# Sigmoid attention and a seven-product MLP: operands and decoding placed anew, 27 rounding copies on ScalarE, one PSUM tile for each bank

## The chip, the cores and the metric

The kernel runs on one core of one Trainium2 chip. The metric is device time in microseconds for one execution of the whole program; the time given for a kernel is the median of its runs. The engines are called as in the profile: PE (TensorE, matmuls), PEld (its weight loads), DVE (VectorE), ACT (ScalarE), POOL (GpSimd) and SP (SyncE, which here issues the DMAs).

## What is computed

Eight batches of 12 heads with 448 tokens and head size 64 go through attention with a sigmoid in place of a softmax; the result, as 3584 tokens of width 768, goes through two linear layers with a gate between them. All arrays are float32.

```
scores = (q @ k.T) / sqrt(64) - log(448)
x      = (1 / (1 + exp(-scores))) @ v          # per batch and head, then [3584, 768]
h      = x @ w_in                              # [3584, 2048]
g      = h * clip(h + 3, 0, 6) / 6
out    = g @ w_out                             # [3584, 768]
```

## The kernel before

**Stages.** Tokens are taken as four pairs of batches, n = 0 to 3. The program runs attention for batches 0 to 3, the first product (`x @ w_in`) for pair 0, attention for batch 4, product for pair 1, attention for batches 5 and 6, product for pair 2, attention for batch 7, product for pair 3, and then the second product (`g @ w_out`) for all four pairs.

**Products.** Each big product is split in two in every dimension and done with seven block products in place of eight; in the code they are P1, P5, P6, P2, P7, P3, P4, and this is also their order in time. Every float32 operand is split in a rounded part and a rest (two tiles of type fp32r), and a block product is three passes over these: high by high, high by low, low by high. One call of `product` is nine matmuls of 448 columns.

**Token operands.** `take` (L219) adds the two PSUM halves of one head pair into a raw tile `xr` (ACT copies one half, DVE adds the other). `put` (L228) makes one operand of the first product from a raw tile: L230 rounds it into x[:, 0], L231 subtracts to get the rest into x[:, 1]. `minus` (L234) is a difference of two raw tiles. For each pair n and each of three columns c, `t_ops` (L237) places seven puts and four differences, with b11, b12, b21, b22 the four raw tiles. In before all of them run on DVE.

**Decoding of weights.** `w_in` and `w_out` arrive as 64-bit numbers. `prep` (L91) decodes one of eight blocks of either (`which` 0 or 1) in two units: a load, an ACT step `head` (L108), five DVE steps (L113 to L123), an add on POOL (L127); then four sums on POOL and seven stores to a DRAM scratch. So there are 32 units. `split_w` (L261) reads weights back (`raw` tiles), rounds them on ACT (L264) and subtracts on DVE (L265).

**One quarter of a first product.** `quads` (L276) runs the seven products for two column blocks i = 0, 1 and four quarters jj. On the way, `seed` (L303, ACT) copies the P1 bank into the P2 bank before P6 goes on adding to P1; `keep` (L307, ACT) saves P5; `seed2` (L311, DVE) writes the P3 bank, and P7 may add to P1 only after it; `h22` (L315, DVE) makes the tile `snh`, and P4 may add to P1 only after it. `gate` (L327, ACT) and `gate2` (L330, DVE) turn four results into g11, g22, g12 and g21; `diff` (L335, DVE) makes the four differences t1 to t4; all are stored for the second product.

**PSUM.** There are eight banks of 512 columns. Four are the tiles pv0 to pv3 (`bank`, L86). The other four are two tiles of two banks each, sc0 and sc1 (`pair_banks`, L80): in attention one step's scores fill such a pair. In the first product each of the four roles P1, P5, P2, P3 needs two banks, one for each i; which role has which banks turns with jj. Two roles have single banks, and two have one pair tile, which holds both i:

```
m = (jj + (P1, P5, P2, P3).index(role)) % 4
if m % 2:
    return bank(f"z_{n}_{jj}_{role}_{i}", (m - 1) + i)
if role not in whole:
    whole[role] = pair_banks(f"z_{n}_{jj}_{role}", turn[0] + m // 2)
return whole[role][:, i]
```

Waits are made per tile, from the accesses that the program records on it.

**Order.** The order of the work is a list: `at(place, f, ...)` gives a step its place, in microseconds of a planned timeline, and the list is sorted by place. PE, DVE, ACT and POOL take their instructions in just that order, and each waits at its first instruction that isn't ready. SP's DMAs are ordered by the compiler's scheduler. In the plan, the four first products begin at places 136.0, 273.1, 443.0 and 580.1 (`marks`), attentions at 5.0, 240.4, 377.5 and 547.3 (`starts`).

Of the kernel before, what the change touches and what calls it, by code (L numbers as in the profile page):

```python
# [43 lines left out]
def tile_kernel(ctx: ExitStack, tc: tile.TileContext, qk, vP, w8, outT):  # L44
# [183 lines left out]
    def put(n, k, c, q):  # L228
        x = one.tile([P, 2, S], F32R, tag=f"x{k}{c}", name=f"x_{n}_{k}_{c}")
        nc.vector.tensor_copy(x[:, 0], xr[q])  # L230
        nc.vector.tensor_tensor(out=x[:, 1], in0=xr[q], in1=x[:, 0].bitcast(F32), op=ALU.subtract)  # L231
        X[n, k, c] = x
# [231 lines left out]
    for n, bs in enumerate(runs):  # L464
        steps = [(b, m, r) for b in bs for m in range(HC) for r in range(LC)]
        lag = 2
        starts.append(now)
# [21 lines left out]
    for n in range(NT):
        free = marks[n - 1] + HF * q if n else 0.0  # L490
        for c in range(HC):
            own = [taken[2 * n + (h % 2), c + HC * (h // 2)] for h in range(4)]
            late = 0.4 * c
            first = (max(free - 11.6 * TU + 1.1 * c, own[0] + late), max(free - 5.6 * TU + 1.1 * c, own[2] + late))
            upper = max(free - 9.6 * TU + 1.7 * c + 0.5, own[1] + late, first[0] + 0.1)
            if max(own) < free:
                both = free - 0.5 + 7 * c
                t_ops(n, c, (first, upper, both), 0.9)
# [62 lines left out]
```

## Time and profile before

| | us |
|---|---|
| runs | 1140.26, 1143.6, 1144.16 |
| median | 1143.6 |
| profiled execution: time | 1146.25 |
| profiled execution: span | 1144.5 |
| PE busy | 1101.1 (96%) |
| DVE busy | 832.2 (73%) |
| ACT busy | 609.8 (53%) |
| POOL busy | 147.3 (13%) |

How to read it: the span is the time from the first to the last instruction. Matmuls are pipelined, so PE counts as busy while any is under way, also when its clock is throttled; the granted clock (PEclk) is a number of its own. A view of groups gives, for each line and form, the count, the busy time, the mean duration in ns of one, and the idle time of the engine just before, with what ended it. A view of waits gives, for each pair of waiter and releaser, the microseconds in total, the times, and the longest. Names in it are without their numbers: z is a PSUM tile of the first product, y and yb those of the second, sc and pv those of attention, x an operand, w a split weight.

### The profile page before, as it was taken

Reading aid. Unit: us, or ns where it says so; the run is one execution under the profiler, and the core shown is the slowest. Engines: PE = TensorE matmul, PEld = TensorE weight load, DVE = VectorE, ACT = ScalarE, POOL = GpSimd, SP = SyncE. Lnnn points to the kernel's source line nnn. Section 1 sums busy time; section 2 is a strip of 40 time slices with the busy share of each in tenths; the row PEclk is TensorE's granted clock in tenths of the full one; section 3 lists DMA queues with packets and bytes.
Section 4 is the critical chain, followed back from the end, with each engine's and each line's share of the span. In section 5 each row is a group of like instructions: output and inputs, shape, how many; then the busy total and the mean of one; then the engine's idle time right before and its main releaser. Section 6 shows DMA issues by size and latency. Waiting matters only on the chain.

```text
span 1144.5 us, 17865 instructions
## 1 busy us (share of the span) xinstructions
PE 1101.1 (96%) x6720; PEld 888.9 (78%) x6720; DVE 832.2 (73%) x1128; ACT 609.8 (53%) x814; POOL 147.3 (13%) x102
## 2 busy tenths in 40 slices
PE   8989999988899989999989999999999999999998
PEld 3436688983488854699854989999999999999997
DVE  4897688999589889668797786856655665665563
ACT  6857844536544457745437354554455445445542
POOL 0533443201212202021130000000000000000000
PEclk9999999989899999999999999999999999999999
DMA  7877899774779767678853987394543453355341
GB/s 267 274 261 252 278 319 312 256 248 179 228 234 301 237 229 239 220 242 265 282 179 115 361 282 227 131 419 169 174 178 125 142 188 131 121 171 170 124 147 68
DMA packets 95270, 250.22 MB, mean 219 GB/s; under 512 B 10576, under 2 KB 66256, under 8 KB 90704
## 3 DMA queue, kind: packets, MB, share of 16 engines
q1 hardware_dynamic: 95040, 249.01, 63.8%
q8 instruction: 53, 0.87, 0.3%
q14 instruction: 33, 0.27, 0.1%
q10 hardware_dynamic: 144, 0.07, 0.0%
HBM read 164.63 MB, written 84.41 MB: 218 GB/s over the span
## 4 chain that ended last, share of the span: by engine, by line
PE 69%; DVE 18%; issue 5%; DMA 4%; ACT 4%; SPq 0%; ACTq 0%; DVEq 0%
PE y L408 24%; PE z L297 19%; PE yb L408 12%; PE sc L188 7%; PE pv L214 6%; DVE w L265 3%; DMA raw<-wd 2%; DVE t L335 2%; DVE x L231 2%; DVE x L230 2%; DVE xr L235 2%; DVE g L330 2%; ACT w L264 1%; PE sc L183 1%; PE pv L208 1%
## 5 line engine op out<-in xcount | busy, mean ns | idle before, releaser
L297 PE MATMUL z<-x,w 128*128 128x448 f32 x2016 | 423.5, 372 | 15.7 <-ACT z L305 7.9
L297 PEld LDWEIGHTS z<-x,w 128*128 128x128 f32 x2016 | 383.4, 191 | 57.1 <-issue 10.8
L408 PE MATMUL y<-x,w 128*128 128x448 f32 x1344 | 308.0, 364 | 0.0
L408 PEld LDWEIGHTS y<-x,w 128*128 128x128 f32 x1344 | 252.0, 187 | 19.9
L265 DVE TENSOR_TENSOR w<-w,w 128x768 fp32r<-128x768 f32 x112 | 107.3, 958 | 153.8 <-ACT w L264 152.5
L194 ACT ACTIVATE a<-sc,bias_s 128x896 f32<-128x896 f32 x168 | 168.9, 1008 | 71.6 <-PE sc L188 39.2
L264 ACT CAST w<-w 128x768 fp32r<-128x768 f32 x112 | 93.4, 834 | 190.8 <-PE yb L408 187.1
L188 PE MATMUL sc<-qk 64*64 64x448 f32 x1152 | 174.8, 557 | 10.0 <-DVE g L330 5.3
L214 PE MATMUL pv<-a,v 64*64 64x448 f32 x1152 | 174.8, 548 | 9.0 <-DVE xr L223 7.6
L408 PE MATMUL yb<-x,w 128*128 128x448 f32 x672 | 172.3, 364 | 0.0
L265 DVE TENSOR_TENSOR w<-raw,w 128x768 fp32r<-128x768 f32 x112 | 126.4, 1132 | 44.5 <-ACT w L264 41.9
L408 PEld LDWEIGHTS yb<-x,w 128*128 128x128 f32 x672 | 126.0, 187 | 9.9
L127 POOL TENSOR_TENSOR wa<-wa,st 128x768 f32<-128x768 f32 x32 | 64.4, 2012 | 448.3 <-DVE st L123 374.3
L391 DVE TENSOR_TENSOR x<-gr,x 128x896 fp32r<-128x896 f32 x112 | 121.5, 1085 | 0.0
L327 ACT ACTIVATE g<-z,bias 128x448 f32<-128x448 f32 x96 | 59.5, 632 | 110.4 <-DVE g L330 55.5
L188 PEld LDWEIGHTS sc<-qk 64*64 64x64 f32 x1152 | 62.9, 136 | 70.7 <-issue 42.7
L214 PEld LDWEIGHTS pv<-a,v 64*64 64x64 f32 x1152 | 65.5, 136 | 67.1 <-issue 43.2
L264 ACT CAST w<-raw 128x768 fp32r<-128x768 f32 x112 | 93.3, 833 | 39.6 <-PE z L297 21.4
L390 ACT CAST x<-gr 128x896 fp32r<-128x896 f32 x112 | 105.3, 941 | 0.0
L330 DVE SCALAR_TENSOR_TENSOR g<-g,z 128x448 f32<-128x448 f32 x96 | 58.9, 615 | 15.3 <-ACT g L327 15.1
L231 DVE TENSOR_TENSOR x<-xr,x 128x448 fp32r<-128x448 f32 x84 | 58.8, 700 | 2.9
L327 ACT ACTIVATE g<-snh,bias 128x448 f32<-128x448 f32 x32 | 21.5, 671 | 71.2 <-DVE snh L317 69.8
(42 smaller groups left out, 687.2 us busy)
## 6 DMA issues: line engine op xcount, KB each, us to landing
gr<-gd SPq DMA_DIRECT2D x28, 1792.0 KB, 7.8
raw<-wd SPq DMA_DIRECT2D x112, 384.0 KB, 4.2
gd<-t SPq DMA_DIRECT2D x128, 224.0 KB, 3.5
gd<-g SPq DMA_DIRECT2D x96, 224.0 KB, 3.8
qk<-qk SPq DMA_DIRECT2D x47, 448.0 KB, 5.6
st<-wi SPq DMA_DIRECT2D x16, 768.0 KB, 5.1
wd<-ws SPq DMA_DIRECT2D x64, 192.0 KB, 4.7
st<-wo SPq DMA_DIRECT2D x16, 768.0 KB, 5.8
```

Source lines behind the costliest of these rows:

```text
L188: nc.tensor.matmul(sc[halves[h], j, :S], k[halves[j], ks], q[halves[j]], start=True, stop=True)
L194: nc.scalar.activation(a, sc[:, :, :S], AF.Sigmoid, bias=bias_s, scale=scale)
L214: nc.tensor.matmul(pv[b, hp][h][halves[j], :S], v[halves[h], j * NC + c], a[halves[h], j], start=c == 0 and not (second and shared), stop= ...
L231: nc.vector.tensor_tensor(out=x[:, 1], in0=xr[q], in1=x[:, 0].bitcast(F32), op=ALU.subtract)
L264: nc.scalar.copy(h, src)
L265: nc.vector.tensor_tensor(out=l, in0=src, in1=h.bitcast(F32), op=ALU.subtract)
L297: nc.tensor.matmul(z[i, k][:, :S], w[:, wu, c * P : (c + 1) * P], X[n, k, c][:, xu], start=m == 0 and k in (P1, P5), stop=m == 3 * HC - 1, ...
L327: nc.scalar.activation(new(i, o), src(i, o), AF.Relu, bias=bias_3, scale=1.0)
L330: nc.vector.scalar_tensor_tensor(out=g[i, o], in0=g[i, o], scalar=6.0, in1=src(i, o), op0=ALU.min, op1=ALU.mult)
L390: nc.scalar.copy(x[:, 0], src)
L391: nc.vector.tensor_tensor(out=x[:, 1], in0=src, in1=x[:, 0].bitcast(F32), op=ALU.subtract)
L408: nc.tensor.matmul(z[k][e][:, :S], w[:, wu, e * P : (e + 1) * P], x[:, xu], start=u == 0 and i == 0 and k in (P1, P5, P2, P3), stop=u == H ...
```

## The change

It does five things.

1. The pair tiles get a pool of their own, opened anew for each attention, each first product and the second product (`open_four`). In a first product its four banks are now four tiles of one bank (z00, z01, z20, z21), so that no two column blocks i share a tile.
2. `put` takes the rounding copy as an argument: 27 of the 84 run on ACT (`nc.scalar.copy`), the others on DVE as before. On ACT are P1 and P5 of pair 1, P1 and P2 of pairs 2 and 3 (in the last quarter of the product before), P3 of pair 1 and P7 and P3 of pair 3 (after their own product has begun). DVE has 1101 instructions in place of 1128, ACT 840 in place of 813.
3. The differences are formed in another order, into other tiles, so that P7 (b12) and P3 (b22) can be made last; for pairs 0 and 2 they stand up to a dozen places behind the others, for pairs 1 and 3 partly in their own product.
4. The places of the operands are set for each pair by hand.
5. The decode blocks get places from a table. For `w_in` they were 11 + 20 j with 10 between a block's two units, and are now 8, 26, 44, 74, 92, 110, 128, 146 with 9; for `w_out` they were 186 + 48 j with 15 between units, and are now given relative to the stages, with 12. In product 0's last quarter and the attention behind it none stands any more; between places 443 and 547 there are six units in place of four.

```
-    def t_ops(n, c, ready, gap):
+    def t_ops(n, c, early, upper, both, late, gap):
...
+        for (place, copy), k, q in zip(early, (P1, P2), (b11, b21)):
+            at(place, put, n, k, c, q, copy)
+        at(upper[0], minus, b11, b12, b11)
+        at(upper[0] + gap / 2, put, n, P5, c, b11, upper[1])
         for i, part in enumerate((
-            (put, n, P3, c, b22), (minus, b12, b22, b12), (minus, b22, b22, b11), (put, n, P6, c, b22), (put, n, P7, c, b12),
-            (minus, b21, b21, b22), (put, n, P4, c, b21),
+            (minus, b11, b22, b11), (put, n, P6, c, b11), (minus, b12, b22, b12), (minus, b21, b21, b11), (put, n, P4, c, b21),
         )):
             at(both + gap * i, *part)
+        for (place, copy), k, q in zip(late, (P7, P3), (b12, b22)):
+            at(place, put, n, k, c, q, copy)
...
-            if role not in whole:
-                whole[role] = pair_banks(f"z_{n}_{jj}_{role}", turn[0] + m // 2)
-            return whole[role][:, i]
+            return four["pool"].tile([P, 512], F32, tag=f"z{m}{i}", name=f"z_{n}_{jj}_{role}_{i}")
...
+            elif n == 1:
+                early = ((free - 11.6 * TU + 2.2 * c, act), (free - 0.5 + 9 * c, dve))
+                upper, both, gap = (free - 9.6 * TU + 3 * c, act), free + 0.7 + 9 * c, 1.2
+                late = ((start - 5 + 1.3 * c, dve), (start + 2 * TU + 1.5 * c, act))
...
+        prep(0, j, (8, 26, 44, 74, 92, 110, 128, 146)[j], 9)
```

**Place 1: ACT at the end of the first quarter of product 0** (from gates to the next quarter's seeds; a z name holds pair, quarter, role, block i and a running number, and that of a pair tile has no block). Before:

```order
L327 ACTIVATE g12_0_0_1_1775<-z_0_0_5_1_1654,bias_3_107 128x448 [waits PE_49]
L264 CAST w_0_2_2_1784<-raw_0_1_2_1657 128x768 [waits DMAHW6_49,Activation_49]
L327 ACTIVATE g21_0_0_0_1799<-z_0_0_0_1547,bias_3_107 128x448 [waits PE_49]
L108 ACTIVATE wa_0_7_1684<-st_0_7_1_1694 128x768 [waits DMAHW0_49]
L327 ACTIVATE g21_0_0_1_1823<-z_0_0_0_1547,bias_3_107 128x448 [waits DVE_49]
L264 CAST w_0_2_3_1831<-raw_0_1_3_1688 128x768 [waits DMAHW7_49,Activation_49]
L305 COPY z_0_1_3_0_1847<-z_0_1_0_0_1813 128x448 [waits PE_49]
L305 COPY z_0_1_3_1_1862<-z_0_1_0_1_1837 128x448 [waits PE_49]
```

Now:

```order
L335 ACTIVATE g12_0_0_1_1788<-z_0_0_5_1_1670,bias_3_107 128x448 [waits PE_49]
L274 CAST w_0_2_2_1797<-raw_0_1_2_1674 128x768 [waits DMAHW7_49,Activation_49]
L335 ACTIVATE g21_0_0_0_1813<-z_0_0_0_0_1561,bias_3_107 128x448 [waits PE_49]
L335 ACTIVATE g21_0_0_1_1836<-z_0_0_0_1_1583,bias_3_107 128x448 [waits DVE_49,PE_49]
L274 CAST w_0_2_3_1844<-raw_0_1_3_1711 128x768 [waits DMAHW4_49,Activation_49]
L313 COPY z_0_1_3_0_1860<-z_0_1_0_0_1826 128x448 [waits PE_49]
L313 COPY z_0_1_3_1_1876<-z_0_1_0_1_1850 128x448 [waits DVE_49,PE_49]
```

Before, both g21 gates read one tile (z_0_0_0_1547), and the second waits for DVE up to gate2 of the first g21. Now they read two tiles, and the second waits for DVE only up to t3 of block 0, whose reading frees the gate's output buffer. The decode step L108 no longer stands between them.

**Place 2: DVE in the last quarter of product 0** (from gate2 of g11 to g22). Before:

```order
L330 SCALAR_TENSOR_TENSOR g_0_3_0_2460<-g_0_3_0_2460,z_3_3_0_2356 128x448
L230 CAST x_3_0_2478<-xr_3_1000 128x448
L231 TENSOR_TENSOR x_3_0_2478<-xr_3_1000,x_3_0_2478 128x448
L330 SCALAR_TENSOR_TENSOR g_0_3_1_2476<-g_0_3_1_2476,z_3_3_1_2374 128x448
L230 CAST x_3_1_2483<-xr_4_1112 128x448
L231 TENSOR_TENSOR x_3_1_2483<-xr_4_1112,x_3_1_2483 128x448
L317 TENSOR_TENSOR snh_3_0_2495<-z_3_0_0_2322,sne_3_0_2394 128x448
L230 CAST x_3_2_2504<-xr_5_1223 128x448
L231 TENSOR_TENSOR x_3_2_2504<-xr_5_1223,x_3_2_2504 128x448
L330 SCALAR_TENSOR_TENSOR g_0_3_0_2502<-g_0_3_0_2502,snh_3_0_2495 128x448
L317 TENSOR_TENSOR snh_3_1_2517<-z_3_0_1_2346,sne_3_1_2408 128x448
L330 SCALAR_TENSOR_TENSOR g_0_3_1_2519<-g_0_3_1_2519,snh_3_1_2517 128x448
```

Now:

```order
L338 SCALAR_TENSOR_TENSOR g_0_3_0_2469<-g_0_3_0_2469,z_3_3_0_2373 128x448
L245 TENSOR_TENSOR xr_2_1180<-xr_2_1529,xr_2_1180 128x448
L241 TENSOR_TENSOR x_1_2_2477<-xr_2_1180,x_1_2_2477 128x448
L338 SCALAR_TENSOR_TENSOR g_0_3_1_2489<-g_0_3_1_2489,z_3_3_1_2387 128x448
L325 TENSOR_TENSOR snh_3_0_2502<-z_3_0_0_2340,sne_3_0_2405 128x448
L338 SCALAR_TENSOR_TENSOR g_0_3_0_2509<-g_0_3_0_2509,snh_3_0_2502 128x448
L325 TENSOR_TENSOR snh_3_1_2521<-z_3_0_1_2363,sne_3_1_2419 128x448
L338 SCALAR_TENSOR_TENSOR g_0_3_1_2523<-g_0_3_1_2523,snh_3_1_2521 128x448
```

The three operands of P2 (x_3_0 to x_3_2) have left this place for the attention behind it; of P5's (x_1_2) only the subtraction L241 is here, its rounding is on ACT.

**Place 3: ACT at the start of the program** (a is a sigmoid's result, wa the first decode block). Before:

```order
L194 ACTIVATE a_0_0_142<-sc_0_0_137,bias_s 128x896
L194 ACTIVATE a_0_1_149<-sc_0_1_144,bias_s 128x896
L194 ACTIVATE a_0_2_160<-sc_0_2_151,bias_s 128x896
L194 ACTIVATE a_0_3_173<-sc_0_3_168,bias_s 128x896
L194 ACTIVATE a_0_4_184<-sc_0_4_179,bias_s 128x896
L108 ACTIVATE wa_0_190<-st_0_0_131 128x768
```

Now:

```order
L204 ACTIVATE a_0_0_145<-sc_0_0_140,bias_s 128x896
L204 ACTIVATE a_0_1_152<-sc_0_1_147,bias_s 128x896
L204 ACTIVATE a_0_2_163<-sc_0_2_154,bias_s 128x896
L118 ACTIVATE wa_0_171<-st_0_0_131 128x768
L204 ACTIVATE a_0_3_180<-sc_0_3_175,bias_s 128x896
L204 ACTIVATE a_0_4_193<-sc_0_4_187,bias_s 128x896
```

The first decode step on ACT stands two sigmoids earlier.

More of the change, by code (lines that the diff above doesn't have):

```diff
@@ L76, in tile_kernel, with open_four @@
     att = ph2.enter_context(tc.tile_pool(name="att", bufs=1, side="right"))
+    four = {}
     turn = [0]
+    def open_four(name):
+        if four:
+            four["stack"].close()
+        four["stack"] = ExitStack()
+        four["pool"] = four["stack"].enter_context(
+            tc.tile_pool(name=name, bufs=1, space=bass.MemoryType.PSUM, reuse_waits="tile")
+        )
+        turn[0] = 0
     def pair_banks(name, i=None):
@@ L83, in pair_banks @@
             turn[0] += 1
-        return ps.tile([P, 2, 512], F32, tag=f"sc{i % 2}", name=name)
+        return four["pool"].tile([P, 2, 512], F32, tag=f"sc{i % 2}", name=name)
     def bank(name, k):
@@ L226, in tile_kernel, with put @@
     X = {}
-    def put(n, k, c, q):
+    def put(n, k, c, q, copy=nc.vector.tensor_copy):
         x = one.tile([P, 2, S], F32R, tag=f"x{k}{c}", name=f"x_{n}_{k}_{c}")
-        nc.vector.tensor_copy(x[:, 0], xr[q])
+        copy(x[:, 0], xr[q])
         nc.vector.tensor_tensor(out=x[:, 1], in0=xr[q], in1=x[:, 0].bitcast(F32), op=ALU.subtract)
@@ L467, in tile_kernel @@
         starts.append(now)
+        at(now - 0.01, open_four, f"psa{n}")
         for i in range(len(steps) + lag):
@@ L485, in tile_kernel @@
         marks.append(now)
+        at(now - 0.01, open_four, f"psm{n}")
         for jj in range(HF // 2):
@@ L488, in tile_kernel @@
             now += 2 * q
-    for n in range(NT):
-        free = marks[n - 1] + HF * q if n else 0.0
-        for c in range(HC):
+    dve, act = nc.vector.tensor_copy, nc.scalar.copy
+    for c in range(HC):
+        for n in range(NT):
             own = [taken[2 * n + (h % 2), c + HC * (h // 2)] for h in range(4)]
[L493 to L498, printed above, removed]
-            else:
-                t_ops(n, c, (first, upper, max(own[3], first[1] + 0.1, upper + 0.1)), 1.0 if n < NT - 1 or c < 2 else 0.01)
-    for j in range(HF):
-        prep(0, j, 11 + 20 * j, 10)
-        prep(1, j, marks[0] + 50 + 48 * j, 15)
+            free = marks[n - 1] + HF * q if n else 0.0
+            start = marks[n]
+            if n == 0:
+                early = ((own[0], dve), (own[2], dve))
+                upper, both, gap = (max(own[1], own[0] + 1.2), dve), own[3] + 0.1, 1.4
+                late = ((own[3] + 11, dve), (own[3] + 12.5, dve))
+            elif n == 1:
+                early = ((free - 11.6 * TU + 2.2 * c, act), (free - 0.5 + 9 * c, dve))
+                upper, both, gap = (free - 9.6 * TU + 3 * c, act), free + 0.7 + 9 * c, 1.2
+                late = ((start - 5 + 1.3 * c, dve), (start + 2 * TU + 1.5 * c, act))
+            else:
+                early = ((free - 11.6 * TU + 2.2 * c, act), (free - 5.6 * TU + 2.2 * c, act))
+                upper, both, gap = (own[1] + 0.1, dve), own[3] + 0.1, 1.2 if n < 3 or c < 2 else 0.1
+                if n == 2:
+                    late = ((start - 30 + 10 * c, dve), (start - 25 + 10 * c, dve))
+                else:
+                    late = ((start + 4 * TU + 1.5 * c, act), (start + 6 * TU + 1.5 * c, act))
+            t_ops(n, c, early, upper, both, late, gap)
+    for j in range(HF):
+        prep(0, j, (8, 26, 44, 74, 92, 110, 128, 146)[j], 9)
+    for j, place in enumerate((
+        marks[0] + 40, marks[1] + 18, marks[1] + 50, starts[2] + 26, starts[2] + 45, marks[2] + 14, marks[2] + 42, marks[2] + 68
+    )):
+        prep(1, j, place, 12)
     at(marks[3] + 6, open_two)
@@ L506, in tile_kernel @@
     first = now
+    at(now - 0.01, open_four, "psy")
     for n in range(NT):
@@ L517, in tile_kernel @@
     todo.sort(key=order)
+    ctx.callback(lambda: four["stack"].close())
     engines = {mybir.EngineType.PE, mybir.EngineType.Activation, mybir.EngineType.DVE, mybir.EngineType.Pool}
```

7 lines of the change are left out of this document (1 added, 6 removed).

## The prediction, on record before the run

> **What bounds the kernel now.** I read the page's first line, then busy time by stage, then what TensorE waited for, then two stalls in the timeline. The profiled execution:
>
> ```profile
> span 1144.5 us, 17865 instructions
> ```
>
> It took 1146.25 us, 1.75 more than its span; the median of the three runs is 1143.6. The next view cuts the span where TensorE changes from attention to first product and back: length, then busy time of PE, PEld, DVE, ACT and POOL, TensorE's granted clock, DMA share, GB/s. The order is attention (batches 0-3), product 0, attention (4), product 1, attention (5, 6), product 2, attention (7), product 3, second product.
>
> ```profile
> 3.70:142.50 138.80, 133.57 (x1336) 69.82 (x1336) 103.86 (x141) 104.60 (x123) 48.02 (x34) 0.98 0.82 269
> 142.50:259.50 117.00, 109.42 (x520) 98.25 (x520) 105.69 (x150) 51.09 (x80) 32.86 (x21) 0.96 0.83 281
> 259.50:303.50 44.00, 35.12 (x320) 14.45 (x320) 38.09 (x59) 26.50 (x31) 9.04 (x6) 0.92 0.63 216
> 303.50:417.00 113.50, 108.86 (x528) 96.22 (x528) 94.21 (x134) 50.40 (x79) 18.75 (x12) 0.98 0.76 248
> 417.00:480.50 63.50, 62.40 (x652) 28.84 (x648) 48.16 (x77) 50.09 (x60) 10.53 (x7) 1.00 0.64 210
> 480.50:590.50 110.00, 106.22 (x520) 96.06 (x520) 90.62 (x134) 49.77 (x79) 20.44 (x12) 0.98 0.76 250
> 590.50:626.50 36.00, 32.23 (x324) 12.62 (x320) 27.55 (x44) 25.80 (x31) 7.34 (x5) 0.95 0.44 152
> 626.50:733.50 107.00, 106.38 (x517) 95.74 (x518) 79.10 (x121) 50.72 (x80) 0.00 (x0) 1.00 0.70 247
> 733.50:1141.00 407.50, 406.89 (x2013) 376.88 (x2011) 244.89 (x276) 199.14 (x256) 0.00 (x0) 1.00 0.47 167
> ```
>
> The second product has neither idle time nor a clock below 1.00: nothing to win, and the change leaves it alone. In the eight stretches before it, length minus PE busy is 5.2, 7.6, 8.9, 4.6, 1.1, 3.8, 3.8 and 0.6 us, 35.6 together. The missing clock (1 minus the granted clock, times the length) is 2.8, 4.7, 3.5, 2.3, 0, 2.2, 1.8 and 0: 17.3. So at most about 53 us can be won, 25 of them in product 0 and the attention behind it, where VectorE is 87 to 90% busy. Who ended TensorE's waits:
>
> ```profile
> PE z L297 <- ACT z L305: 7.9, 4, 3.3
> PE pv L214 <- DVE xr L223: 7.6, 4, 4.7
> PE z L297 <- DVE z L313: 5.8, 3, 2.2
> PE sc L188 <- DVE g L330: 5.3, 2, 3.7
> PE pv L208 <- DVE xr L223: 4.0, 2, 2.9
> ```
>
> Nearly all are VectorE being late. The first, a seed copy on ScalarE, is one too; these rows show the case of 180 us (ACT twice, DVE twice, PE, then a clock row):
>
> ```profile
> 179.06 0.63 ACT L327 ACTIVATE g<-z,bias 128x448 f32<-128x448 f32 x1 [6.13 <-DVE g L330]
> 180.32 0.96 ACT L305 COPY z<-z 128x448 f32<-128x448 f32 x2
> 174.75 0.62 DVE L335 TENSOR_TENSOR t<-g,g 128x448 f32<-128x448 f32 x1
> 178.42 0.61 DVE L330 SCALAR_TENSOR_TENSOR g<-g,z 128x448 f32<-128x448 f32 x1
> 180.91 3.46 PE L297 MATMUL z<-x,w 128*128 128x448 f32 x10 [2.15 <-ACT z L305]
> 181.00:185.00 4.00, 4.00 (x13) 3.60 (x14) 3.89 (x7) 2.64 (x5) 0.00 (x0) 0.59 0.98 354
> ```
>
> ScalarE stood 6.1 us in front of the second g21 gate until VectorE had finished with the first g21, because both lie in one pair tile. Behind it in ScalarE's queue stood the seeds, and TensorE lost 2.15 us and then clock.
>
> **The change part by part.** The durations, from the groups of VectorE by form, and one of ScalarE:
>
> ```profile
> L265 DVE TENSOR_TENSOR w<-raw,w 128x768 fp32r<-128x768 f32 x112 | 126.4, 1132 | 44.5 <-ACT w L264 41.9 <-DMA raw<-wd 0.7
> L231 DVE TENSOR_TENSOR x<-xr,x 128x448 fp32r<-128x448 f32 x84 | 58.8, 700 | 2.9
> L230 DVE CAST x<-xr 128x448 fp32r<-128x448 f32 x84 | 41.7, 496 | 1.4
> L235 DVE TENSOR_TENSOR xr<-xr,xr 128x448 f32<-128x448 f32 x48 | 37.4, 779 | 0.3
> L117 DVE SCALAR_TENSOR_TENSOR wa<-st,wa 128x768 int32<-128x768 int32 x32 | 33.9, 1059 | 0.3
> L123 DVE SCALAR_TENSOR_TENSOR st<-st 128x768 f32<-128x768 uint32 x32 | 31.2, 976 | 0.5
> L223 DVE TENSOR_TENSOR xr<-pv,xr 128x448 f32<-128x448 f32 x48 | 29.8, 620 | 33.4 <-ACT xr L222 33.4
> L115 DVE TENSOR_SCALAR wa<-wa 128x768 int32<-128x768 int32 x32 | 20.5, 640 | 0.4
> L113 DVE TENSOR_SCALAR wa<-wa 128x768 f32<-128x768 f32 x32 | 20.4, 639 | 23.8 <-ACT wa L108 23.8
> L121 DVE TENSOR_SCALAR st<-wa 128x768 int32<-128x768 int32 x32 | 18.2, 568 | 1.0
> L309 ACT COPY sne<-z 128x448 f32<-128x448 f32 x32 | 16.3, 539 | 9.3 <-PE z L297 9.3
> ```
>
> An operand (put) costs VectorE 0.496 + 0.700 = 1.20 us, a subtraction 0.78, the add of a take 0.62, and one of the 32 decode units 0.639 + 0.640 + 1.059 + 0.568 + 0.976 = 3.88. 27 roundings go to ScalarE: 13.4 us less on VectorE, 27 x 0.539 = 14.6 more on ScalarE. That is hidden by ScalarE's idle half in the products (51 of 117 us busy), and costs up to those 14.6 where TensorE waits behind it. The Trainium skill, "ScalarE: Activation LUTs", section "Rules for kernel authors", gives cheap elementwise work to VectorE, not ScalarE; its formula (186 ns and 0.833 ns per element) makes 0.56 us of such a copy, an estimate, which the row of 0.539 bears out; by that rule the move is a loss of 1.7 us of engine time, while the rows say that only VectorE's time is short.
>
> Three of the 27 (P5's operands of product 1) wait on ScalarE for a subtraction on VectorE. Behind them in its queue stand split copies, which TensorE needs 5.3 products later: a product is nine matmuls at 406.89 / 2013 = 0.202 us, so 9.6 us, less 1.13 for the subtract and about as much for the copy. VectorE may be 7 us late before that shows.
>
> *First attention.* TensorE starts a step every 1.51 us (last two rows). The first sigmoid and decode steps on ScalarE, and the decode's loads:
>
> ```profile
> 9.72 1.01 ACT L194 ACTIVATE a<-sc,bias_s 128x896 f32<-128x896 f32 x1 [0.53 <-PE sc L183]
> 12.16 0.90 ACT L108 ACTIVATE wa<-st 128x768 f32<-128x768 f32 x1
> L98 SPq DMA_DIRECT2D st<-wi x2: 432/459/486, 3.1 to 6.4; - x2
> DMA to landing us min/median/max: 7.5/8.6/9.6
> 11.69 0.94 PE L188 MATMUL sc<-qk 64*64 64x448 f32 x8
> 13.20 0.94 PE L188 MATMUL sc<-qk 64*64 64x448 f32 x8
> ```
>
> For batch 1 each group of seven steps (10.6 us) brings five puts, four subtractions and two adds: 5.98 + 3.12 + 1.24 = 10.3 us. Among the three groups (places 47 to 80 of the table) stood 16 decode operations, 12.6 us. That makes 31.0 + 12.6 = 43.6 in 31.7 us, 11.9 of backlog; 8.0 were lost, so 3.9 are free (an attention bank is wanted again only three steps after its take). The new table has 12 decode operations there (9.4 us) and the last column's P7 and P3 behind it (-2.4): 38.0, 6.3 of backlog, 2.4 beyond the slack, with 1 of clock 3.4. New is a stall: the first decode's ScalarE step now stands ahead of the fourth sigmoid, and its data lands at 3.1 + 7.5 = 10.6, so that sigmoid moves from 9.72 to 11.5 and ends at 12.5; the scores of 11.69, which reuse its bank pair, wait 0.8. Left: 4.2 of 8.0.
>
> *Product 0 and the attention behind it* (24.7 lost). With a tile per bank the second g21 gate waits for t3 of the first half, done at 175.4 instead of 179.0; the seeds come 3.7 us earlier and the 2.15 and their clock (about 1.6) go. In the last quarter and the attention behind it stood 21 puts; now 12 there, 6 with VectorE's subtract alone and 3 behind: 25.1 against 14.4 + 4.2 = 18.6. Two decode units (7.8) leave. 14.3 us of backlog less, from the place where the longest waits (4.7 and 3.3) stand. Left: 24.7 - 3.8 - 14.3 = 6.6.
>
> *Product 1* (6.9): as many decode units as before, six casts fewer (3.0), and no backlog brought along. Left 3.5, half: the mutual waits of VectorE and ScalarE stay. *Attention 5, 6* (1.1): the units fit its idle time. Left 1.5.
>
> *Product 2* (6.0): six decode units instead of four, +7.8, minus six casts, 3.0: VectorE goes from 90.6 to 95.4 us. Against it the tile per bank frees TensorE's P7 of the first half from the second half's seed2. I take 5.5, nearest to today's row. *Attention 7* (5.6): six puts (7.2) leave it, and a unit at its edge. Left 1.5. *Product 3* (0.6): six subtractions of operands more, 4.2, in 107 us of which VectorE works 79. Left 1.0.
>
> Sum left: 4.2 + 6.6 + 3.5 + 1.5 + 5.5 + 1.5 + 1.0 = 23.8 of 52.9, a gain of 29.1. The profiled execution would take 1117, the median 1143.6 - 29.1 = 1114.5.
>
> Bounds of what is left: below, near what the unhurried stretches lose today (1.1 and 0.6): 1, 3 (two stretches), 1, 1, 2, 0 and 0.5, together 8.5. Above: today's 8.0; 14 (only the banks and half of the backlog help); today's 6.9; 4; 12.3, which product 0 lost with VectorE 90% busy; today's 5.6; 3. They won't all come. Less than nothing can't be left, since idle time and missing clock are all that the sum counts.
>
> At nothing I cost the pools opened anew at each stage: the same eight banks, waited for tile by tile. The cover is that the first bank asked for belongs to a role that ends early; without it each of four changes of stage could cost what `PE sc <- DVE g` shows, 3.7 at most. SP carries the same transfers in another order; TensorE's waits on loads are each below the five rows above. DMA, 0.83 busy in product 0, would need 0.93 in a stretch of 104 us.
>
> **The rivals.** *More goes* (all low bounds, 8.5 left): gain 44, 1099. For it speaks that the waits feed each other, ScalarE's on VectorE and back; against it VectorE's untouched 82% in product 2.
>
> *The clock stays full*: the waits left are short, and if only those above 3.4 us (4.7 and 3.7 in the rows) cost clock, the clock's share of what is left goes, 23.8 x 17.3 / 52.9 = 7.8 us: 1106.7. Against it, 0.59 stands behind a wait of 2.15. The Trainium skill, "TensorE: Matmul & The Clock Gate", section "What's actually happening", has this rule: the clock falls after an idle window of about 3.4 us; the trace differs here.
>
> *The backlog moves into product 2*: it loses 12.3 as product 0 did, attention 7 keeps 5.6 and product 1 its 6.9: 6.8 + 4.1 + 3.4 = 14.3 given back, 1128.8. The added units speak for it, the tile per bank against.
>
> *DMA decides the products*: they keep their lengths and all that the attentions win is given back at the next raw load; 1143. Against it, ScalarE's queue waited for raw loads only twice:
>
> ```profile
> ACT w L264 <- DMA raw<-wd: 8.1, 2, 4.2
> ```
>
> *Hand-overs* (slower): each moved rounding makes VectorE's subtract wait for ScalarE, as the split weights do:
>
> ```profile
> DVE w L265 <- ACT w L264: 194.4, 119, 4.7
> ```
>
> At that mean, 194.4 / 119 = 1.63 us, 27 of them idle VectorE for 44 us at its fullest places: 29 gained, 44 lost, 1158.5. It decides if VectorE gets to the subtract before ScalarE has copied; against it, in the first product such a wait is 41.9 / 112 = 0.37 us, and a late VectorE arrives after the copy.
>
> **How the numbers follow.** Forecast (1107 to 1122): 0.51; clock full: 0.05; more goes: 0.17; product 2: 0.16; DMA: 0.04; hand-overs: 0.07. About 0.5% can be told from no change. Faster 0.51 + 0.05 + 0.17 + 0.16 = 0.89, same 0.04, slower 0.07. The range reaches from "more goes" to just beyond "product 2", 1099 to 1130, and leaves out the last two and the tails.
>
> **What would show it.** Right: the 6.1 us wait for `DVE g` at the gate gone from product 0; `PE pv <- DVE xr` from 11.6 us to under 4; product 0 near 108 us and its attention near 35; a new wait of about 0.8 us of TensorE for a sigmoid near 12 us; product 2 still near 110. Wrong: products as long as now with ScalarE waiting for raw; VectorE's subtract of an operand waiting over 1 us for its cast; or idle time of TensorE before 733 us still above 30.

## The result and the profile after

The changed kernel takes 1115.64 us (median of 4 runs, 1115.4 to 1117.07); the kernel before took 1143.28 beside it. The ratio is 0.9764, 95% interval 0.9749 to 0.9778. The profiled execution took 1117.07 us, its span is 1115.2.

The stretches of the changed kernel up to the second product, cut and ordered as in the prediction (length, then PE, PEld, DVE, ACT, POOL, granted clock, DMA share, GB/s):

```profile
3.70:134.90 131.20, 129.06 (x1336) 67.60 (x1336) 103.76 (x141) 104.43 (x123) 52.43 (x36) 1.00 0.86 290
134.90:243.60 108.70, 105.18 (x515) 95.73 (x512) 100.03 (x139) 53.63 (x85) 29.88 (x18) 0.98 0.87 300
243.60:275.70 32.10, 31.72 (x331) 12.49 (x329) 24.59 (x46) 25.45 (x30) 0.00 (x0) 1.00 0.58 191
275.70:383.00 107.30, 104.84 (x514) 95.98 (x512) 90.09 (x131) 53.57 (x87) 18.68 (x12) 0.98 0.77 258
383.00:448.50 65.50, 64.04 (x666) 25.77 (x664) 52.54 (x82) 51.96 (x61) 10.39 (x7) 1.00 0.62 198
448.50:564.50 116.00, 109.07 (x512) 98.07 (x512) 104.18 (x140) 53.80 (x86) 37.36 (x23) 0.96 0.84 284
564.50:596.40 31.90, 31.48 (x330) 12.35 (x328) 19.37 (x34) 25.38 (x30) 0.00 (x0) 1.00 0.38 124
596.40:704.20 107.80, 104.75 (x517) 95.62 (x518) 77.47 (x120) 53.75 (x86) 0.00 (x0) 1.00 0.69 244
```

Seven stretches lost less than was forecast, or at most 2.1 us more (length minus PE busy, plus the missing clock). The sixth, product 2, is not one of them: it was to stay at 110 us and grew to 116, with VectorE at 104.18 us instead of 95.4 and the lowest clock, 0.96. Who ended TensorE's waits now, leaving aside the program's first loads:

```profile
PE z L305 <- DVE z L321: 12.8, 5, 4.7
PE sc L198 <- ACT a L204: 1.7, 4, 0.6
PE pv L224 <- DVE xr L233: 1.3, 2, 1.1
PE pv L224 <- ACT a L204: 1.2, 4, 0.5
PE z L305 <- DVE w L275: 1.2, 1, 1.2
```

Waits for an attention bank (`DVE xr`) fell from 11.6 to 1.3 us, those for the seed copies on ScalarE are gone from the list, and one kind stands out: the seed2 of line 321, with 12.8 us where before had 5.8. Its longest case, at the end of product 2, row by row (start, duration; GpSimd, VectorE, TensorE):

```profile
547.37 2.47 POOL L137 TENSOR_TENSOR wa<-wa,st 128x768 f32<-128x768 f32 x1 [12.16 <-DVE st L133]
546.33 0.96 DVE L133 SCALAR_TENSOR_TENSOR st<-st 128x768 f32<-128x768 uint32 x1
547.21 0.95 DVE L275 TENSOR_TENSOR w<-raw,w 128x768 fp32r<-128x768 f32 x1
548.07 2.25 DVE L241 TENSOR_TENSOR x<-xr,x 128x448 fp32r<-128x448 f32 x1
550.25 1.15 DVE L321 TENSOR_TENSOR z<-z,sne 128x448 f32<-128x448 f32 x2
551.01 2.21 PE L305 MATMUL z<-x,w 128*128 128x448 f32 x5 [4.72 <-DVE z L321]
```

Ahead of seed2 in VectorE's queue stand a decode unit's operations, a split and an operand's subtraction, and the last took 2.25 us while a GpSimd add of 2.47 us was running; the median of such a subtraction is 0.62.

### The profile page after: what moved, and what is told of

It is laid out like the page before. It is cut to its first block, busy times and chain, and to the rows that moved or that the text cites. A ratio compares the mean times of both kernels' runs of the same rounds, so it can differ in the third digit from the quotient of the medians.

```text
span 1115.2 us, 17907 instructions
## 1 busy us (share of the span) xinstructions
PE 1087.1 (97%) x6720; PEld 880.5 (79%) x6720; DVE 816.8 (73%) x1101; ACT 622.2 (56%) x841; POOL 149.1 (13%) x102
## 4 chain that ended last, share of the span: by engine, by line
PE 73%; DVE 10%; DMA 8%; issue 5%; POOL 2%; ACT 2%; SPq 0%; ACTq 0%; DVEq 0%; POOLq 0%
PE y L416 24%; PE z L305 20%; PE yb L416 12%; PE sc L198 7%; PE pv L224 7%; DMA raw<-wd 2%; DVE w L275 2%; DMA gr<-gd 2%; POOL ws L146 1%; PE sc L193 1%; DVE t L343 1%; DMA st<-wi 1%; PE pv L218 1%; DVE g L338 1%; POOL wa L137 1%
## 5 line engine op out<-in xcount | busy, mean ns | idle before, releaser
L305 PE MATMUL z<-x,w 128*128 128x448 f32 x2016 | 420.5, 371 | 14.8 <-DVE z L321 12.8
L198 PE MATMUL sc<-qk 64*64 64x448 f32 x1152 | 149.5, 544 | 5.5 <-DMA qk<-qk 3.7
L224 PE MATMUL pv<-a,v 64*64 64x448 f32 x1152 | 149.6, 537 | 3.5 <-DVE xr L233 1.3
L398 ACT CAST x<-gr 128x896 fp32r<-128x896 f32 x112 | 104.9, 937 | 6.5 <-DMA gr<-gd 6.5
L198 PEld LDWEIGHTS sc<-qk 64*64 64x64 f32 x1152 | 53.5, 134 | 66.0 <-issue 43.4
L224 PEld LDWEIGHTS pv<-a,v 64*64 64x64 f32 x1152 | 54.3, 133 | 61.7 <-issue 47.2
L241 DVE TENSOR_TENSOR x<-xr,x 128x448 fp32r<-128x448 f32 x84 | 56.8, 678 | 8.5 <-ACT x L240 6.4
```

The costliest lines, as they stand in the source:

```text
L198: nc.tensor.matmul(sc[halves[h], j, :S], k[halves[j], ks], q[halves[j]], start=True, stop=True)
L224: nc.tensor.matmul(pv[b, hp][h][halves[j], :S], v[halves[h], j * NC + c], a[halves[h], j], start=c == 0 and not (second and shared), stop= ...
L305: nc.tensor.matmul(z[i, k][:, :S], w[:, wu, c * P : (c + 1) * P], X[n, k, c][:, xu], start=m == 0 and k in (P1, P5), stop=m == 3 * HC - 1, ...
L398: nc.scalar.copy(x[:, 0], src)
```

## The experiments

All are compared with runs of the kernel before on the same chip. The stage lengths, from the first matmul of a stage to that of the next (us; att for attention, p for first product), come from each kernel's trace, which is one execution; the times are medians. The kernel before took 1142.75 to 1144.68 us on the chips used, so a difference of 2 us between kernels that ran on different chips shows nothing:

| kernel | att 0-3 | p 0 | att 4 | p 1 | att 5, 6 | p 2 | att 7 | p 3 | time | ratio, 95% |
|---|---|---|---|---|---|---|---|---|---|---|
| before | 140.2 | 114.4 | 46.1 | 111.1 | 65.9 | 108.2 | 37.8 | 105.0 | 1143.3 | 1 |
| changed | 132.6 | 107.7 | 32.8 | 106.4 | 66.4 | 115.1 | 32.8 | 105.8 | 1115.64 | 0.9764 (0.9749-0.9778) |
| s1 banks only | 139.6 | 113.1 | 45.7 | 111.1 | 65.9 | 103.6 | 38.4 | 102.4 | 1137.65 | 0.9951 (0.9936-0.9966) |
| s2 pair tiles | 133.1 | 109.0 | 32.8 | 110.2 | 66.4 | 114.8 | 33.6 | 105.7 | 1122.68 | 0.9822 (0.9805-0.984) |
| s3 copies on VectorE | 132.6 | 107.7 | 32.8 | 107.4 | 66.4 | 116.9 | 32.8 | 105.7 | 1119.32 | 0.9789 (0.9775-0.9804) |
| s4 old decode | 136.2 | 108.8 | 36.5 | 109.9 | 64.8 | 104.4 | 36.7 | 105.1 | 1119.83 | 0.9793 (0.9778-0.9807) |
| s5 old operands | 135.2 | 108.7 | 34.1 | 107.2 | 65.8 | 114.1 | 32.8 | 102.2 | 1117.82 | 0.9767 (0.9751-0.9783) |
| s9 decode only | 134.1 | 110.1 | 34.0 | 110.6 | 65.7 | 115.2 | 34.1 | 104.0 | 1124.83 | 0.9843 (0.9824-0.9861) |
| s6 unit late | 133.8 | 106.7 | 32.8 | 106.0 | 66.4 | 106.4 | 32.9 | 106.5 | 1108.95 | 0.9695 (0.9669-0.9722) |
| s7 GpSimd out of 3 blocks | 132.7 | 107.1 | 32.8 | 105.8 | 66.4 | 104.9 | 32.8 | 106.9 | 1107.85 | 0.9683 (0.9668-0.9698) |
| s8 sums on VectorE | 132.6 | 105.4 | 32.8 | 103.8 | 64.7 | 111.5 | 33.3 | 105.5 | 1109.05 | 0.9693 (0.9673-0.9713) |
| s10 s6 and s8 | 133.2 | 106.2 | 32.8 | 104.0 | 64.7 | 105.7 | 33.1 | 105.9 | 1101.8 | 0.9642 (0.9622-0.9662) |
| s11 s10, old operands | 135.3 | 107.2 | 34.1 | 105.3 | 64.7 | 104.7 | 32.8 | 105.5 | 1106.11 | 0.9679 (0.9659-0.97) |
| s12 s10, early operands | 132.0 | 105.9 | 32.8 | 104.0 | 64.7 | 105.0 | 33.1 | 102.9 | 1097.9 | 0.9598 (0.9584-0.9611) |

### s1: only the banks

```
-            if role not in whole:
-                whole[role] = pair_banks(f"z_{n}_{jj}_{role}", turn[0] + m // 2)
-            return whole[role][:, i]
+            return four["pool"].tile([P, 512], F32, tag=f"z{m}{i}", name=f"z_{n}_{jj}_{role}_{i}")
```

(and `open_four`, as in the change.)

> The kernel before with one edit: each half of a product role gets its own one-bank tile; decode, operands and copies stay as before. Theory (VectorE's backlog, shed by the new places of operands and decode, is most of the gain; the banks are a small part): the 6.1 us gate wait of product 0 goes and with it about 4 us, perhaps 1 us more in each of products 1 and 2: 1136 to 1140 us, against 1143.3 before. Rival (false waits by the shared pair tile were what held VectorE and ScalarE up everywhere): 1122 or less, most of the 27.6 us won.

1137.65 us: 5.1 below the 1142.75 of before beside it, as the theory had it. But the place is another: product 0 won 1.3 us, product 2 4.6 and product 3 2.6. Of the last, 2.0 is not a wait that the banks removed but the pace of the matmuls, which has two values (last section).

### s2: everything but the banks

The reverse edit in the changed kernel.

> The changed kernel with the pair tiles of before in the first product and everything else of the change. Theory: 3 to 6 us slower than the changed kernel, 1119 to 1122 us, and the long gate wait is seen again. Rival (the banks are most of it): 1135 or more. Third outcome: no difference, 1115 to 1117, since the places of operands and decode already made VectorE early enough that the shared tile is free when the second half wants it.

1122.68, 7.0 us slower, a little more than expected. ScalarE's gate waits for gate2 on VectorE are back (ScalarE's waits up to the second product, total, times, longest):

```profile
ACT g L337 <- DVE g L340: 67.9, 23, 7.2
```

In the changed kernel that wait comes once, for 1.4 us; in its place the gates wait for the differences of line 343, a third as long. Their largest wait, the one for `snh`, is longer than in s2. The changed kernel, then s2:

```profile
ACT g L335 <- DVE t L343: 22.8, 7, 4.9
ACT g L335 <- DVE snh L325: 75.1, 29, 8.1
```

```profile
ACT g L337 <- DVE snh L327: 58.7, 30, 3.9
```

So ScalarE's gates wait 99 us for VectorE instead of 127. What TensorE feels of it is the seed copies behind the gates, a row that the changed kernel doesn't have (s2's waits of TensorE):

```profile
PE z L307 <- ACT z L315: 8.5, 6, 3.0
```

Over half of the 7 us is lost in product 1 (106.4 to 110.2).

### s3: the rounding copies back on VectorE

```
-    dve, act = nc.vector.tensor_copy, nc.scalar.copy
+    dve, act = nc.vector.tensor_copy, nc.vector.tensor_copy
```

> The changed kernel with all 27 rounding copies back on VectorE at the same places. They are 27 x 0.496 = 13.4 us of VectorE's time, of which 6 copies (3.0 us) stand late in product 0, 6 (3.0) at each end of products 1 and 2, and the others within products. Theory (VectorE's time is short at some of these places): about half of it shows, 4 to 8 us slower, 1120 to 1124 us. Rival (the copies are the gain): 1129 us or more, all 13.4 and its clock. Rival (hand-overs from ScalarE to VectorE cost as much as they save): 1112 to 1116.

1119.32: 3.7 us slower, just below the theory's range. It falls in products 1 and 2 alone (1.0 and 1.8 us), and in product 1 TensorE waits only 0.6 us longer, while the pace of its matmuls takes 1.5. Of 13.4 us that ScalarE took over from VectorE, 3.7 counted at most. Both rivals are out; VectorE waited little for the handed-over copies in the changed kernel (its waits):

```profile
DVE x L241 <- ACT x L240: 6.4, 7, 1.2
```

### s4 and s5: one half of the new order each

s4 puts the decode back:

```
-        prep(0, j, (8, 26, 44, 74, 92, 110, 128, 146)[j], 9)
-    for j, place in enumerate((
...
-        prep(1, j, place, 12)
+        prep(0, j, 11 + 20 * j, 10)
+        prep(1, j, marks[0] + 50 + 48 * j, 15)
```

> The changed kernel with before's places for the 16 decode units; operands, copies and banks of the change stay. Theory: product 2 loses its six units and gains back about 5 us (its 115.1 us fall to about 109), but product 0 and the attention behind it have two units (7.8 us of VectorE) more and the first attention four decode steps more among batch 1's operands: 8 to 11 us lost there. Net 1118 to 1123 us. Rival (the operands did everything, the new decode places only cost): 1108 to 1112 us. Rival (the decode places are the whole gain): 1135 or more.

s5 keeps the new decode, and has `put`, `t_ops` and its places as before the change.

> The changed kernel with before's operand part (its order of puts and subtractions, its places, all casts on VectorE); the decode places and the one-bank tiles of the change stay. Theory (the operands' new places and copies carry most of the gain): banks alone gave 1137.65, banks with new operands 1119.83, so the operands are worth about 18 us and this kernel takes 1130 to 1136. Rival (the decode places do as much without the operands, since both shed the same backlog): 1122 to 1127. Rival (new decode places only pay once the operands have moved): 1137 or more.

s4 took 1119.83, inside the theory's range. Product 2 wins more than expected (115.1 to 104.4), and the others lose more: 3.6 + 1.1 + 3.7 us up to attention 4, as expected, but 3.5 in product 1 and 3.9 in attention 7 besides. s5 took 1117.82, and there the theory fell: the operand part was to be worth 18 us, and without it the kernel loses 2, which the intervals can't tell from nothing. 1117.82 is below even the range of the rival that it bears out, the decode places doing as much (1122 to 1127). With the banks in place the four combinations are 1137.65 (both old), 1119.83 (operands new), 1117.82 (decode new) and 1115.64 (both new). Either half takes away nearly the whole backlog. Attention 4 shows it: 45.7 us with both old, 36.5 and 34.1 with one new, and 32.8 with both.

### s9: only the decode places

In the kernel before, the two calls of `prep` get the new table and its gaps, as in the change.

> The kernel before with one edit: the new places and gaps of the 16 decode units; pair tiles, operands and copies as before. New theory after the runs so far (one backlog, which either the decode places or the operand places take away; with both the second finds little left): 1117.82 was measured with the banks as well, and the pair tiles cost the changed kernel 7 us, so 1121 to 1127 us. Old theory (the operands carry most): 1132 or more. Rival (the decode places work only with one-bank tiles): 1130 or more, with the long gate waits.

1124.83: 18 us of the 28 come from a table of 16 numbers and two gaps, without new operands, copies or banks. Its step to s5 (1117.82) prices the banks once more, at 7.0 (8.7 by the ratios, since the two ran on different chips).

### s6 and s7: why product 2 grew

```
-        marks[0] + 40, marks[1] + 18, marks[1] + 50, starts[2] + 26, starts[2] + 45, marks[2] + 14, marks[2] + 42, marks[2] + 68
+        marks[0] + 40, marks[1] + 18, marks[1] + 50, starts[2] + 26, starts[2] + 45, marks[2] + 14, marks[2] + 42, starts[3] + 2
...
-        prep(1, j, place, 12)
+        prep(1, j, place, 9 if j == 7 else 12)
```

> The changed kernel with the last decode unit of w_out moved from product 2 into the last attention (starts[3] + 2, its halves 9 apart). Theory (product 2 is longer only because of the decode units in it): product 2 falls from 115.1 us to 107 to 109, the last attention rises by at most 2 of its 32.8: 1108 to 1112 us. Rival (the last attention has no room: its takes come late and ScalarE's sigmoids behind the decode steps): 1114 to 1118, the time only moves. Rival (product 2 is long for another reason, such as the casts or DMA): product 2 stays above 112.

s7 leaves the units in product 2 and takes GpSimd's part out of those of the last three blocks; it leaves out work that the result needs:

```
-            else:
+            elif which == 0 or j < 5:
                 nc.gpsimd.tensor_tensor(out=a, in0=a, in1=e, op=ALU.add)
...
+        bare = which == 1 and j >= 5
-        for i in range(4):
+        for i in range(0 if bare else 4):
             at(place + gap + 10.5 + 1.3 * i, sums, i)
...
-        at(place + gap + 17, store, "s", (P5, P6, P7, P3))
+        at(place + gap + 17, store, "a" if bare else "s", (P5, P6, P7, P3))
```

> The changed kernel without GpSimd's work in the last three w_out decode units (the add of the low part and the four sums are left out, the four plain blocks are stored in the sums' place), so that part of the second weight is not what the reference uses; VectorE's decode steps, ScalarE's and the DMAs stay. In the trace, VectorE operations that overlap a GpSimd add in product 2 take up to 2.3 us instead of 0.62. Theory A (product 2's loss is VectorE held up by GpSimd): VectorE's busy time there falls from 104.2 by 7 to 10 us, product 2 to 107 to 110, 1108 to 1111 us. Theory B (the loss is the units' own work on VectorE, 3.9 us each): product 2 stays at 113 or more, 1113 to 1116 us.

Product 2 from its first matmul to that of attention 7, in the changed kernel:

```profile
449.60:564.70 115.10, 108.39 (x508) 97.87 (x505) 103.25 (x139) 53.64 (x85) 37.36 (x23) 0.96 0.84 284
```

in s6:

```profile
449.50:555.90 106.40, 103.55 (x508) 94.40 (x504) 91.42 (x127) 52.12 (x83) 27.13 (x17) 1.00 0.85 290
```

and in s7:

```profile
448.40:553.20 104.80, 104.32 (x508) 94.45 (x504) 89.99 (x136) 53.70 (x85) 7.17 (x5) 1.00 0.90 306
```

s6 took 1108.95: 8.7 us of product 2 go with one block's units, a little more than expected, and the last attention takes them for 0.1. s7 took 1107.85: VectorE executes nearly the same operations there (136 against 139) but is busy 90.0 us instead of 103.3. Summed over product 2, VectorE's operations are longer than the medians of their forms by 13.8 us in the changed kernel, by 6.0 in before and by 2.0 in s7. So theory A, and by more than each of its three ranges: product 2 grew because GpSimd's adds hold VectorE up, by some 12 us (the rest of the 13.3 is three operations fewer). VectorE's own work on the units, still there, costs nothing that shows: 104.9 us is about what s4 needs with fewer units (104.4).

### s8: the adds on VectorE

```
-                nc.gpsimd.tensor_tensor(out=a, in0=a, in1=e, op=ALU.add)
+                nc.vector.tensor_tensor(out=a, in0=a, in1=e, op=ALU.add)
...
-            nc.gpsimd.tensor_tensor(out=o, in0=x, in1=y, op=op)
+            nc.vector.tensor_tensor(out=o, in0=x, in1=y, op=op)
```

> The changed kernel with all of the decode's adds on VectorE instead of GpSimd (32 of 128x768, 64 of 128x384). By the trace they would take VectorE about 32 x 1.06 + 64 x 0.55 = 69 us; 68 VectorE operations that overlap a GpSimd add are now longer than their median by 64 us in all. Theory (GpSimd's adds cost VectorE about their own price already): within 5 us of the changed kernel, 1111 to 1120. Rival (the lengthened operations mostly lie where VectorE is idle anyway, and the moved ones do not): 1122 or more. Rival (the hold-ups are worse than the work, since they come at random places): 1110 or less.

1109.05, 6.6 us less than the changed kernel: the second rival, not my theory. The busy times of the changed kernel,

```profile
PE 1087.1 (97%) x6720; PEld 880.5 (79%) x6720; DVE 816.8 (73%) x1101; ACT 622.2 (56%) x841; POOL 149.1 (13%) x102
```

those of s8, and its adds:

```profile
PE 1080.8 (98%) x6720; PEld 864.0 (78%) x6720; DVE 813.2 (74%) x1197; ACT 621.0 (56%) x841; POOL 0.3 (0%) x6
...
L137 DVE TENSOR_TENSOR wa<-wa,st 128x768 f32<-128x768 f32 x32 | 30.6, 955 | 0.5
L146 DVE TENSOR_TENSOR ws<-wa 128x384 f32<-128x384 f32 x32 | 17.7, 552 | 0.0
L146 DVE TENSOR_TENSOR ws<-wa,ws 128x384 f32<-128x384 f32 x16 | 8.8, 553 | 0.0
L146 DVE TENSOR_TENSOR ws<-ws,wa 128x384 f32<-128x384 f32 x16 | 8.8, 553 | 0.1
```

96 more operations, and VectorE is busy 3.6 us *less*: giving the adds to GpSimd had saved VectorE nothing. Busy time counts an overlap once, and an operation begins about 0.08 us before the one ahead of it ends (above, 548.07 against 547.21 + 0.95), so prices are better compared by durations. Summed so, VectorE's operations take 872.6 us in the changed kernel and 878.1 in s8, 65.9 of them the adds. The adds on GpSimd had been costing VectorE 872.6 - (878.1 - 65.9) = 60.4 us, about as much as doing them. Why the move then wins 6.6 us was not tested by itself; my reading is that a hold-up falls on whatever operation is next, seed2 among them, and a queued add where the table puts it.

### s10 and s11: both gains, and the operands once more

> The changed kernel with both edits that gained: the last decode unit in the last attention, and all of the decode's adds on VectorE. Theory (they act at different places but for product 2: the first won 8.7 us in product 2 of 115.1, the second 2.3, 2.6, 1.7 and 3.6 us in product 0, product 1, attention 5 and 6 and product 2): 1099 to 1104 us. Rival (in the last attention the adds on VectorE delay the takes): attention 7 above 35, 1105 to 1110. Rival (one VectorE lack that either removes, as with operands and decode): 1106 to 1109.

> As the kernel with both gains (last decode unit in the last attention, decode's adds on VectorE), but with before's operand part: its order of puts and subtractions, its places, all casts on VectorE. With the changed kernel's decode the old operands were within 0.2% (1117.82 against 1115.64). Theory (the operand part matters little once decode is moved): 1100 to 1108, within 4 us of the other. Rival (with six puts and a decode unit in the last attention VectorE falls behind there): attention 7 above 38, 1110 or more. Rival (its product 3, 102.2 us instead of 105.8, makes it the faster one): 1097 to 1100.

s10 has the edits of s6 and s8 and took 1101.8, as the sum of the two said; the last attention stays at 33.1. s11 took 1106.11, inside its theory's range but 4.3 us from s10 and so just over its bound of 4: with the decode out of the way the operand part is worth about 4 us. The rival on product 3 fell with it: 105.5, no better than s10 (TensorE waits 1.2 us there, half of it for this product's own operands).

### s12: why product 3 did not gain

```
-                    late = ((start + 4 * TU + 1.5 * c, act), (start + 6 * TU + 1.5 * c, act))
+                    late = ((max(start - 1 + 0.8 * c, own[3] + 0.6), act), (start + 1.5 + 0.8 * c, act))
```

> As the kernel with both gains (last decode unit in the last attention, decode's adds on VectorE), and the last two operands of product 3 (P7 and P3 of each column) right at its start instead of 4 and 6 products into it. What it tests: in every kernel with the new operand part the second product's first loads (two of 1.8 MB, two of 1.5 MB) leave only 15 to 17 us after product 3 begins and within 4 us of each other, ScalarE's split copy then waits 11 to 13 us for its raw blocks, and TensorE loses 2 us to a seed2 behind that; with the old operands they leave at 4.7 and 11.3 us, and product 3 took 102.2 and 102.4. Theory (the late operands hold the attention's buffers, so those loads bunch): they leave before 8 us, the raw waits fall below 6 us, product 3 from 105.9 to 102 to 104, 1097 to 1100 us. Rival (product 3 is longer for VectorE's six more subtracts of operands): loads earlier but product 3 stays above 105, 1101 to 1103. Rival (ScalarE's six copies at the start hold up the split copies and TensorE there): product 3 above 106, 1103 or more.

When the second product's first loads leave, in the changed kernel (product 3 begins at 597.5):

```profile
612.37 0.42 SPq L391 DMA_DIRECT2D gr<-gd  x1
612.85 0.45 SPq L386 DMA_DIRECT2D w<-wd  x1
614.09 0.44 SPq L391 DMA_DIRECT2D gr<-gd  x1
616.29 0.63 SPq L386 DMA_DIRECT2D w<-wd  x1
```

and in s12 (begins at 581.2):

```profile
585.85 0.38 SPq L391 DMA_DIRECT2D gr<-gd  x1
586.28 0.42 SPq L386 DMA_DIRECT2D w<-wd  x1
592.68 0.43 SPq L391 DMA_DIRECT2D gr<-gd  x1
593.16 0.42 SPq L386 DMA_DIRECT2D w<-wd  x1
```

ScalarE's waits for raw blocks in product 3, changed kernel, then s12:

```profile
ACT w L274 <- DMA raw<-wd: 12.1, 4, 3.5
```

```profile
ACT w L274 <- DMA raw<-wd: 5.0, 1, 5.0
```

As the theory said: at 4.7 and 11.5 us into the product instead of 14.9 to 18.8, product 3 from 105.9 to 102.9, 1097.9 us in all. What the runs don't show is that early loads are enough. Before, s9 and s11 have the old operands and their first loads leave early too (4.7 to 7.7 and 11.3 to 14.4 us in), yet product 3 takes 104.0 to 105.5 us there: s11 has the waits of TensorE just named, before the slower pace of the matmuls (2.0 us, last section), and s9 a wait of 0.9 us and 0.7 us of pace.

s12 is faster than the kernel before and than the changed one: ratio 0.9598 (0.9584 to 0.9611) to before, and 0.9598 / 0.9764 = 0.983 to the changed kernel, the intervals being far apart.

## Why the prediction was right, and where not

The forecast of 1114.5 us and the mechanism (VectorE's backlog in front of TensorE, gone) held up to product 2. The 6.1 us gate wait is gone, product 0 is near 108, its attention below 35; "product 2 still near 110" did not come. That the total is 1.1 us off is luck, since its terms are further off: by stage lengths the gains were 7.6 us in the first attention (3.8 forecast), 20.0 in product 0 and the attention behind it (18.1), 4.7 in product 1 (3.4), 5.0 in attention 7 (4.1), and -6.9 in product 2 (+0.5). What product 2 lost against the forecast, 7.4, these others happened to win (3.8 + 1.9 + 1.3 + 0.9). The sum's ledger is rough too: by the rows of after 20.4 us of idle time and about 9 of clock are left, 29 and not 23.8, though the span fell by 29.3; some 6 us of the gain had been counted as busy time.

- *First attention*: the step "2.4 beyond the slack" was wrong: of the waits for xr one of 0.2 us is left (2.1 us of all kinds, 4.2 forecast). The new stall is there: the decode's step stands before two sigmoids (first fence, ScalarE), and the scores wait (second, TensorE), 0.6 where 0.8 was forecast.

```profile
10.35 0.92 ACT L118 ACTIVATE wa<-st 128x768 f32<-128x768 f32 x1 [1.38 <-DMA st<-wi]
11.17 1.88 ACT L204 ACTIVATE a<-sc,bias_s 128x896 f32<-128x896 f32 x2
```

```profile
12.21 0.98 PE L198 MATMUL sc<-qk 64*64 64x448 f32 x8 [0.59 <-ACT a L204]
```

- *Product 0 and the attention behind it*: 6.1 left, 6.6 forecast, by a sum whose parts don't add. 3.8 for the banks was 1.3 in s1 and in s2 (without the pace of the matmuls 2.0 and 0.1). 14.3 of backlog, from operands and decode together, is nearly taken away by either (s4, s5): once attention 4 is at 32.8 us there is no more to win.
- *Product 1*: 4.6 left, 3.5 forecast. Most of its gain needs the banks (s2), to which the sum gives a price in product 0 alone.
- *Product 2*: the failed step is "six decode units instead of four, +7.8 [...] VectorE goes from 90.6 to 95.4 us", and with it "I take 5.5". 11.6 are left. A unit was priced by VectorE's instructions alone, 3.88 us. What was left out is its adds on GpSimd, which hold VectorE up (s7, s8) and in this stretch went from 12 to 23 (GpSimd's count in the rows). VectorE's excess over the medians there went from 6.0 to 13.8 us: 7.9 more, 95.4 + 7.9 = 103.3, and 104.18 was measured. 11.6 is about the size that the rival "The backlog moves into product 2" gave to this stage (12.3, by a VectorE 90% busy, as it now was); but it named the added units as the reason, not their adds, and what it took back in attention 7 and product 1 did not come.
- *Product 3*: 1.0 forecast, 3.1 left, and for another reason: not six subtractions, but "SP carries the same transfers in another order", costed at nothing. The late operands hold the attention's buffers, four big loads leave within 4 us, the raw blocks queue behind them, and VectorE's split, waiting for ScalarE's, keeps seed2 behind it (s12). In the changed kernel's product 3, ScalarE once and VectorE twice; TensorE's wait of 2.10 us for this seed2 is in the last section:

```profile
637.50 0.83 ACT L274 CAST w<-raw 128x768 fp32r<-128x768 f32 x1 [3.55 <-DMA raw<-wd]
638.36 0.96 DVE L275 TENSOR_TENSOR w<-raw,w 128x768 fp32r<-128x768 f32 x1 [4.29 <-ACT w L274]
639.24 1.16 DVE L321 TENSOR_TENSOR z<-z,sne 128x448 f32<-128x448 f32 x2
```

- *Hand-overs* fell (s3; 6.4 us of waits instead of 44), and so did "the clock stays full", below. The 1099 of "more goes" needed three further edits: s12 reached it.

What stays open: where all of the 6 us between ledger and span lie (2.3 are the matmuls' pace, which takes 3.6 us in before and 1.3 in the changed kernel), why the adds on VectorE win 6.6 us, and whether the operand part alone is worth anything in the changed kernel (2 us, inside the intervals).

## What to carry to other kernels

When two edits shed the same backlog, their prices don't add: test each alone before crediting either, and the cheapest may do most of it (here a table of 16 places, 18 of 28 us). Price a moved piece of work with what it does to its neighbours: its adds on another engine, the buffers that it holds, the loads that wait for them. In a queue served in order look for the operation with the least slack, here seed2, and keep whatever has time to spare from standing ahead of it.

## What the runs showed of the hardware

*VectorE beside GpSimd.* In the changed kernel 66 VectorE operations that overlap a GpSimd add are over 0.3 us longer than the median of their form, by 59 us in all (the expectation of s8 has 68 and 64); no other operation of VectorE is. A split by itself takes 0.95 us, beside an add up to 2.6. The Trainium skill, "SBUF — State Buffer", section "Who interferes with whom", says that a VectorE instruction with two SBUF inputs contends with a GpSimd instruction that reads SBUF, and calls the port pair that the two engines share an exclusive lock. The trace agrees, with 2.25 us for the subtraction of 0.62 above.

*The clock.* After 78 waits of TensorE between 0.8 and 1.82 us (all 14 kernels here, from the first loads to the second product) the granted clock of the next 6 us never fell below 0.9; after 28 waits from 1.84 to 2.75 us it did 12 times; after 18 from 2.87 us on, each time. The changed kernel has both cases: two of its waits, and the 6 us behind each (the clock is the third number from the end).

```profile
518.96 1.34 PE L305 MATMUL z<-x,w 128*128 128x448 f32 x3 [1.97 <-DVE z L321]
640.01 7.53 PE L305 MATMUL z<-x,w 128*128 128x448 f32 x36 [2.10 <-DVE z L321]
```

```profile
519.00:525.00 6.00, 6.00 (x22) 5.43 (x23) 6.00 (x7) 0.65 (x1) 5.84 (x5) 0.72 0.94 277
640.00:646.00 6.00, 5.99 (x30) 5.58 (x31) 2.42 (x4) 2.12 (x4) 0.00 (x0) 1.00 1.03 380
```

0.72 over 6 us is 1.7 us lost, nearly as much as the wait itself. Up to 1.8 us a wait cost no clock, from 2.9 on it always did, and between the two its length did not decide. In the prediction I read the rule of the Trainium skill ("TensorE: Matmul & The Clock Gate", "What's actually happening": the clock falls after an idle window of about 3.4 us) against one wait of 2.15 and wrote that the trace differs. The tally bears that out: the clock fell after 20 waits of under 3.4 us.

*Two paces of matmuls.* With no wait and a granted clock of 1.00, the matmuls of the first products follow each other either every 202.6 ns or every 206.6. Here are 35 us of product 3 of before, then of s1; the first count in brackets is TensorE's matmuls.

```profile
665.00:700.00 35.00, 35.00 (x171) 31.80 (x170) 23.31 (x35) 15.27 (x24) 0.00 (x0) 1.00 0.71 235
```

```profile
660.00:695.00 35.00, 35.00 (x175) 32.44 (x174) 23.40 (x36) 17.24 (x27) 0.00 (x0) 1.00 0.73 245
```

A pace holds until TensorE is next interrupted: of 201 uninterrupted stretches of 18 matmuls or more, in all 14 traces, none has both. The slower one costs up to 2.0 us of a product's 504 matmuls, and 1.1 to 4.8 us of a kernel; it shows neither as idle time nor as missing clock. What decides between the two no run here shows. So a difference of up to 2 us between the same product of two kernels need not come from the edit.
